# Dense products between attention passes: one fixed issue order, weights transposed in place, three w1 slabs used twice

## The chip, the cores and the metric

The kernel runs on one core of a Trainium2 chip. The metric is the device time of one execution in microseconds (us). Each quoted time is the median of several runs, and all runs that are compared here are of the same (fast) state. A core has these engines: PE (TensorE, matrix products and transposes), DVE (VectorE), ACT (ScalarE), POOL (GpSimd) and SP (SyncE, which here issues the loads); sixteen DMA engines move the data. Each engine works through its own list of instructions, and the engines wait for each other through semaphores.

## The reference

Two identical layers, each an attention of one query over a cache of 65536 keys, followed by a feed-forward block; the outputs are the result and the gradients of all inputs.

```python
# D = 1024, 32 query heads, 4 key/value heads of 128, cache 65536, F = 3584, all bf16
x = A_x
x = x + attention(layernorm(x), A_k_cache, A_v_cache, A_wq, A_wo)
x = x + (relu(layernorm(x) @ B_w1 + B_b1) ** 2) @ B_w2 + B_b2
x = x + attention(...)        # the same weights and caches again
x = x + feed_forward(...)
# returned: x, and the vector-Jacobian product with grad_out for all nine inputs
```

The two caches have 67 MB each, so the work is four passes over them (forward of layer 1, forward of layer 2, and two backward passes), and between the passes there are three short **dense stretches** in which vectors are multiplied by wq, wo, w1 and w2. A pass cannot finish its arithmetic without the vectors that the stretch before it produces.

## The kernel before

All loads go into slots of one arena in SBUF, the core's on-chip memory (a slot has 8 KB per partition, and holds one slab of w1 or four rows of w2 or wq). A load is issued into a slot only when what was read from it is done. So if the reader of a slab is late, a load is late too. Between two passes seven or eight cache blocks are also kept in slots for the next pass.

A product of a vector with the *rows* of a weight needs the weight transposed. This is done in pieces: PE transposes eight 128x128 blocks into PSUM, the memory that takes PE's results (`front`), ACT or DVE copies the piece to SBUF (`evac`), and PE multiplies it by the vector (`back`). Some pieces are instead multiplied directly by DVE (one `scalar_tensor_tensor`), to share the work. Pieces that are transposed and not yet multiplied wait in a queue:

```python
class Rows:                                   # kernel before, shortened
    def front(self, job, kc, slab):           # for each piece:
        if stt <= tra:                        #   DVE is less loaded: a direct product
            nc.vector.scalar_tensor_tensor(...)
            self.did(job)
            continue
        pt = self.ps_wt()                     #   else PE transposes it
        for i in range(w):
            nc.tensor.transpose(pt[:, i, :], job["cols"](slab, k0 + i), ident_b[:, :])
        wt = self.pool.tile([P, 8, P], BF, name="wt", tag="wt", bufs=self.bufs)   # bufs = 6
        evac(wt[:, 0:w, :], pt[:, 0:w, :])
        self.queue.append((job, kc, q, wt))
        if len(self.queue) >= self.bufs:
            yield
    # ... back(): eight matmuls with the oldest piece of the queue
    def fill(self):
        while len(self.queue) < self.bufs and next(self.feed, "end") != "end":
            pass
    def run(self):
        self.fill()
        while self.queue:
            self.back()
            self.fill()                       # the queue is filled up to six after every product
```

The passes are held to program order (`with tc.manual_schedule(engines=ORDERED): pipeline(...)`, for PE, DVE and ACT in passes 1 to 3). The dense stretches are not: there the compiler's scheduler may move an instruction ahead of others on the same engine.

## Time and profile before

| | before |
|---|---|
| time, median (range) of the runs beside the changed kernel | 2032.6 us (2026.9 to 2035.4, 4 runs) |
| span of the profiled run | 2027.6 us |
| bytes moved by DMA | 794.98 MB |
| DMA rate inside the passes, median of the 149 windows of 10 us away from the stretches, the start and the end | 421 GB/s (118 of them 410 to 428) |
| granted PE clock, mean of the run | 0.904 |

From the page of the kernel before: the granted PE clock and the DMA rate in 40 equal slices of about 51 us, and the DMA total.

```profile
PEclk9989899799999987898998989889888889798888
...
GB/s 389 420 420 420 419 423 397 371 362 420 420 418 420 420 399 279 352 420 421 420 417 412 401 267 266 370 410 423 422 420 421 393 423 396 363 402 423 421 379 245
DMA packets 110846, 794.98 MB, mean 392 GB/s; under 512 B 9425, under 2 KB 9439, under 8 KB 49375
```

The kernel is bound by DMA in the passes. The rate falls in slices 16 and 17, 24 to 26 and, less, 8 and 9: the dense stretches.

### The profile page before, as it was taken

How to read it: one execution, taken by the hardware profiler on the slowest of the kernel's cores; microseconds unless marked ns; L12 is line 12 of the kernel's file. 1: busy time of each engine (PE TensorE's matmuls, PEld its weight loads, DVE VectorE, ACT ScalarE, POOL GpSimd, SP SyncE). 2: the span in 40 equal slices, each digit the busy share in tenths (PEclk: the TensorE clock that was granted, in tenths of full speed). 3: DMA queues.
4: the chain of work that ended last, by engine and by line, in shares of the span. 5: the costliest groups of instructions: out<-in, count | busy, mean ns of one | idle time of the engine just before them, and what ended most of it. 6: DMA issues, size and time to landing. Idle time of an engine off the chain costs nothing. (4 is left out here: it accounts for less than half of the span.)

```text
span 2027.6 us, 67015 instructions
## 1 busy us (share of the span) xinstructions
PE 1626.9 (80%) x30210; PEld 1332.9 (66%) x30210; DVE 1174.3 (58%) x2358; ACT 1044.6 (52%) x1613; POOL 144.5 (7%) x332
## 2 busy tenths in 40 slices
PE   6877888687877877787787887788788888698896
PEld 6877777687777776786676885455455555355554
DVE  5645455245554543544454457677667777577675
ACT  3434344144344352435363445587667667577675
POOL 0000000000000000000000001112121111111111
PEclk9989899799999987898998989889888889798888
DMA  9999999989999997899999977999999999999996
GB/s 389 420 420 420 419 423 397 371 362 420 420 418 420 420 399 279 352 420 421 420 417 412 401 267 266 370 410 423 422 420 421 393 423 396 363 402 423 421 379 245
DMA packets 110846, 794.98 MB, mean 392 GB/s; under 512 B 9425, under 2 KB 9439, under 8 KB 49375
## 3 DMA queue, kind: packets, MB, share of 16 engines
q1 hardware_dynamic: 86510, 624.99, 75.7%
q0 software_dynamic: 24048, 165.70, 19.8%
q8 instruction: 236, 3.87, 0.8%
q14 instruction: 52, 0.42, 0.1%
HBM read 624.96 MB, written 165.69 MB: 390 GB/s over the span
## 5 line engine op out<-in xcount | busy, mean ns | idle before, releaser
L153 DVE COPY kt<-ps_tr 128x1024 bf16<-128x1024 bf16 x724 | 497.8, 689 | 473.8 <-PE ps_tr L913 256.7
L150 ACT CAST arena<-ps_gg 128x1024 bf16<-128x1024 f32 x452 | 439.9, 1009 | 219.0 <-PE ps_gg L1280 160.7
L913 PE MATMUL ps_tr<-ident_b,arena 128*128 128x128 bf16 x3840 | 310.2, 226 | 60.4 <-DMA arena<-in_A_k_cache_dram 45.1
L913 PEld LDWEIGHTS <-arena 128*128 128x128 bf16 x3840 | 234.0, 101 | 66.6 <-DMA arena<-in_A_k_cache_dram 48.1
L153 DVE CAST arena<-ps_gg 128x1024 bf16<-128x1024 f32 (+1 forms) x191 | 228.9, 1198 | 82.4 <-PE ps_gg L1280 48.0
L150 ACT COPY kt<-ps_tr 128x1024 bf16<-128x1024 bf16 x164 | 172.2, 1054 | 183.9 <-PE ps_tr L1105 126.0
L1280 PE MATMUL ps_gg<-GG,xt 64*128 64x512 bf16 x1024 | 211.6, 413 | 46.4 <-DVE arena L153 26.8
L1015 PE MATMUL ps_acc<-arena 128*128 128x64 bf16 (+4 forms) x4096 | 206.0, 196 | 45.7 <-DMA arena<-in_A_v_cache_dram 31.7
L1226 PE MATMUL ps_tr<-ident_b,arena 128*128 128x128 bf16 x1824 | 175.9, 234 | 35.3 <-DMA arena<-in_A_v_cache_dram 34.4
L931 PE MATMUL ps_sc<-L_qpad,kt 128*128 128x64 bf16 (+7 forms) x3584 | 183.4, 194 | 17.9 <-issue 11.5
L996 ACT ACTIVATE arena<-S_sb,L_negm 128x128 bf16<-128x128 f32 x256 | 165.4, 1002 | 57.8 <-DVE L_negm L981 57.7
L1105 PE MATMUL ps_tr<-ident_b,arena 128*128 128x128 bf16 x1920 | 156.3, 228 | 48.3 <-DMA arena<-in_A_v_cache_dram 48.3
L1015 PEld LDWEIGHTS <-arena 128*128 128x128 bf16 x4096 | 159.8, 100 | 50.0 <-DMA arena<-in_A_v_cache_dram 34.8
L1226 PEld LDWEIGHTS <-arena 128*128 128x128 bf16 x1824 | 119.5, 104 | 88.8 <-issue 49.6
L931 PEld LDWEIGHTS <-kt 128*128 128x128 bf16 x3584 | 153.3, 100 | 23.6 <-issue 14.6
L1105 PEld LDWEIGHTS <-arena 128*128 128x128 bf16 x1920 | 118.6, 102 | 52.2 <-DMA arena<-in_A_v_cache_dram 51.0
L1306 PE MATMUL ps_acc<-X,arena 128*128 128x64 bf16 (+3 forms) x2048 | 119.7, 199 | 24.8 <-DMA arena<-in_A_k_cache_dram 24.8
L996 ACT ACTIVATION_READ_ACCUMULATOR arena<-S_sb,L_negm 128x1 f32 x256 | 127.8, 499 | 0.0
L1306 PEld LDWEIGHTS <-arena 128*128 128x128 bf16 x2048 | 87.1, 102 | 59.9 <-issue 33.1
L1150 PE MATMUL ps_acc<-dsT,arena 128*128 128x64 bf16 (+7 forms) x2048 | 103.7, 195 | 20.0 <-DMA arena<-in_A_k_cache_dram 15.8
L1280 PEld LDWEIGHTS <-xt 64*128 64x128 bf16 x1024 | 61.3, 94 | 86.3 <-issue 46.8
L1259 PE MATMUL ps_sc<-DOB,kt 128*128 128x64 bf16 (+3 forms) x1824 | 117.5, 200 | 0.0
(266 smaller groups left out, 2169.3 us busy)
## 6 DMA issues: line engine op xcount, KB each, us to landing
arena<-in_A_k_cache_dram SPq DMA_DIRECT2D x86, 2048.0 KB, 21.5
arena<-in_A_v_cache_dram SPq DMA_DIRECT2D x83, 2048.0 KB, 21.4
out_dram<-arena POOLq DMA_DIRECT2D x151, 1024.0 KB, 11.4
arena<-in_A_v_cache_dram SPq DMA_DIRECT2D x76, 1024.0 KB, 16.5
arena<-in_A_k_cache_dram SPq DMA_DIRECT2D x76, 1024.0 KB, 16.8
arena<-in_B_w_dram SPq DMA_DIRECT2D x32, 896.0 KB, 5.8
arena<-in_A_wq_dram SPq DMA_DIRECT2D x22, 1024.0 KB, 13.8
arena<-in_A_wo_dram SPq DMA_DIRECT2D x18, 1024.0 KB, 17.5
```

Source lines behind the costliest of these rows:

```text
L150: nc.scalar.copy(out=out, in_=in_)
L153: nc.vector.tensor_copy(out=out, in_=in_)
L913: nc.tensor.transpose(pt[:, i, :], kb8[:, i, :], ident_b[:, :])
L931: nc.tensor.matmul(state["ps_s"][:, s:s + w, :].rearrange("p a b -> p (a b)"), lhsT=kt[:, i, :], rhs=L["qpad"][:, g, 0:w, :].rearrange("p ...
L996: nc.scalar.activation(out=E(p, g, c0, SU)[:, :, h], in_=S[:, h, :], func=ACTF.Exp, bias=L["negm"][:, g, su, h:h + 1], scale=SCALE, accum_ ...
L1015: nc.tensor.matmul(ps_o[:, 0:w, :], lhsT=vb8[:, i, :], rhs=E(p, g, c, w), start=(c % SU == 0), stop=(c % SU == SU - 1), skip_group_check=True)
L1105: nc.tensor.transpose(pt[:, i, :], vb8[:, i, :], ident_b[:, :])
L1150: nc.tensor.matmul(ps_dq[:, 0:w, :].rearrange("p a b -> p (a b)"), lhsT=kb8[:, i, :], rhs=dsT[:, s:s + w, :].rearrange("p a b -> p (a b)") ...
L1226: nc.tensor.transpose(pt[:, i, :], vb8[:, i, :], ident_b[:, :])
L1259: nc.tensor.matmul(state["ps_dp"][:, s:s + w, :].rearrange("p a b -> p (a b)"), lhsT=vt[:, i, :], rhs=DOB[:, g, 0:w, :].rearrange("p a b - ...
L1280: nc.tensor.matmul(pg[:, 512 * h:512 * h + 512], lhsT=xt[64 * h:64 * h + 64, j1 // 8 + m, :], rhs=gg[64 * h:64 * h + 64, :, :].rearrange(" ...
L1306: nc.tensor.matmul(ps_dq[:, 0:w, :].rearrange("p a b -> p (a b)"), lhsT=kb8[:, i, :], rhs=X[:, s:s + w, :].rearrange("p a b -> p (a b)"), ...
```

## The change

The intent: (1) keep three of the eight w1 slabs of the forward product for the backward product that follows, which saves 2.75 MB of loads; (2) write the transposed piece back into its own slab, which saves six buffers; (3) hold the dense stretches to program order too, with the small vector steps spread among the transposes, and put the first transposes of the third stretch between the last steps of pass 3. In the first stretch four more pieces are multiplied directly by DVE (18 instead of 14). The core of the diff:

```diff
+    ordered.enter_context(tc.manual_schedule(engines=ORDERED))     # now around everything up to pass 4
@@ Rows.front
                 if stt <= tra:
                     nc.vector.scalar_tensor_tensor(...)
                     self.did(job)
+                    yield
                     continue
-                wt = self.pool.tile([P, 8, P], BF, name="wt", tag="wt", bufs=self.bufs)
-                evac(wt[:, 0:w, :], pt[:, 0:w, :])
-                self.queue.append((job, kc, q, wt))
-                if len(self.queue) >= self.bufs:
-                    yield
+                wt = slab[:, k0 * P:(k0 + w) * P].rearrange("p (a b) -> p a b", b=P)
+                evac(wt, pt[:, 0:w, :])
+                sl.users += 1                      # the slab stays occupied until back()
+                self.queue.append((job, kc, q, wt, sl))
+                yield
@@ Rows
-    def run(self):
-        self.fill()
-        while self.queue:
-            self.back()
-            self.fill()
+    def step(self):                                # AHEAD = 3
+        if self.chain is not None and next(self.chain, "end") == "end":
+            self.chain = None
+        for _ in range(2):
+            if self.queue and self.queue[0][0]["ready"] and (_ == 0 or len(self.queue) > self.AHEAD):
+                self.back()
+        r = self.one()                             # one piece: a transpose or a direct DVE product
+        return self.chain is not None or self.queue or r is None
+    def run(self, known=True):
+        # ... known: products of the first weight at once; else: self.fill(2)
+        while self.step():
+            pass
@@ second stretch
-    run(g_w1(L4, ps_mv, pre=rows.fill))
-    rows.run()
+    w1a, w1b = w1_twice(3)                         # three slabs stay for the second product
+    run(g_w1(L4, ps_mv, it=w1a))
+    rows.run(False)
@@ pass 3 and third stretch
-    attn_bwd3(2, L3, on3, bg, [(10, pre_load("wq3", ...))])
+    attn_bwd3(2, L3, on3, bg, [(10, begin34)] + [(k, lambda: rows34.fill(1)) for k in range(8, 0, -1)])
# ... (cut: first stretch, generators for the layer norms)
```

## The prediction

> **What bounds the kernel now.** The page's slices show DMA at 9 tenths or more nearly everywhere: 795 MB at a mean of 392 GB/s. Inside the four attention passes the stretches run at 418 to 428 GB/s. At 421 GB/s the bytes alone take an estimated 1888 us of the 2028 us span. The Trainium skill, "DMA: Bandwidth & Descriptors", Specifications, gives a fabric ceiling of 435 GB/s and this trace agrees. The other 140 us are stretches where the queue has no free slot. From 10 us windows, counted as time lost against 421 GB/s: first to second pass (330 to 440 us) 15 us, second to third (760 to 850) 25 us, third to fourth (1150 to 1320) 46 us, end of the last pass 28 us, the rest scattered. Only the three dense stretches, 86 us, can be helped.
>
> **What limits the dense stretches.** The timeline of 793.9 to 824.6 us (w1 backward, then wo) takes 31 us; 8 transposes take 0.46 us and 8 following matmuls 0.25 us, so its 228 + 228 PE instructions are an estimated 20 us of PE work. PE waits there for copies of transposed weights and for w1 loads. From 1175 to 1234.5 us PE does an estimated 47 us (8 side matmuls 0.42 us) in 60 us.
>
> **What the change does.**
> 1. Three of 16 w1 loads go: 2.75 MB, an estimated 6.5 us of DMA, in the second stretch, where they are waited for.
> 2. Transposed weights go back into their slab. Slabs stay occupied until their matmuls are issued, so about 1.5 slots of buffering (six 256 KB tiles) are lost. The copies' number and cost stay (DVE 0.69, ACT 1.01 us).
> 3. The order is fixed: transposes and matmuls alternate at a depth of two to three pieces, about 1.4 us apart, enough for a 1.01 us copy; layernorm chains run among transposes of the next weights. The skill ("TensorE: Matmul & The Clock Gate", Architectural detail) calls ACT and DVE strict FIFO, so a fixed order can also stall; untested here.
> 4. By the instruction order, PE work hardly changes: third stretch 428 to 416 transposes, second 228 as before; the first has 80 instead of 112, with 18 instead of 14 direct DVE products (1.30 us each), so DVE takes over there at about 23 us. All 64 wq transposes move into the tail of pass 3. Pass 4 keeps its order. The start stall of passes 3 and 4 (kept blocks fill the slots; DMA 107 to 163 GB/s at 1230 to 1250 us) moves but stays.
>
> **On the critical path.** A transition that PE leaves earlier ends the DMA pause earlier, so the gain is the shortening: first 2 us, second 8 us (6.5 us of loads and most of the waits, overlapping), third 8 us of at most 13. Sum 18 to 20 us.
>
> **Predicted: 2011 us, range 1994 to 2026.** Faster by over 2%: 0.07; within 2%: 0.91; slower by over 2%: 0.02.
>
> **What would show it.** DMA total 792.2 MB; pass rates unchanged at about 420 GB/s; the w1 backward and wo stretch 22 to 24 us instead of 31; the third stretch (from the end of pass 3's last matmul to the first dO) about 52 instead of 60 us; the first nearly unchanged; the pause at the start of pass 4 still 15 to 20 us.
>
> **What would make it wrong.** Lost buffering: if slabs held stop the loads, the third stretch gains nothing (2020 us). Early transposes may wait behind late loads and delay pass 3's matmuls. If the fixed order removes the start pauses of passes 3 and 4 too, 1990 us or less.

## More of the kernel before

I count **lost DMA time** as the sum over 20 us windows of (window) x (1 - rate / 421 GB/s). Counted to the last whole microsecond of the span, it comes to 138.6 us before the change: 25.8 us between 740 and 880 us (the second stretch, before pass 3), 47.3 us between 1140 and 1360 us (the third stretch and the start of pass 4), and 65.5 us elsewhere. Lost time plus bytes / 421 GB/s is the span by construction (but for the last fraction of a microsecond), so a table of lost time tells where a change of the span came from, and not why.

The two stretches as windows of the trace. After the window and its length the columns are busy us (and count) of PE, PE weight loads, DVE, ACT and POOL, then the granted PE clock, the DMA share and GB/s.

```profile
core 0: us, PE busy (x) PEld busy (x) DVE busy (x) ACT busy (x) POOL busy (x), PEclk, DMA share, GB/s
793.00:825.00 32.00, 27.10 (x487) 24.63 (x487) 22.34 (x58) 17.82 (x22) 0.61 (x13) 0.91 0.88 323
1175.00:1236.00 61.00, 56.37 (x1085) 53.86 (x1085) 42.71 (x106) 35.33 (x41) 1.83 (x12) 0.95 0.75 278
```

PE is the busiest engine there, at 85% and 92%. What it does in the third stretch, from the timeline of PE (L631 is a transpose of a piece, L656 the products of a piece, L1553 a forward product with the same w2 slab):

```profile
start us, us, engine line op out<-in xcount [idle before <-releaser]
...
1201.07 0.64 PE L631 MATMUL ps_sc<-ident_b,arena 128*128 128x128 bf16 x8
1201.54 0.41 PE L656 MATMUL ps_bg<-vcb,wt 128*128 128x64 bf16 x8
1201.79 1.05 PE L1553 MATMUL ps_acc<-L_gb,arena 128*128 128x64 bf16 x16
1202.65 0.64 PE L631 MATMUL ps_sc<-ident_b,arena 128*128 128x128 bf16 x8
...
```

One piece takes 1.58 us (from 1201.07 to 1202.65), and no line has an idle time in brackets: PE never waits for a copy, since the piece multiplied at 1201.54 was transposed and copied earlier. The waits of PE confirm it. The columns are: written tile and line <- releaser, us in total, times, longest; first the second stretch (780 to 870 us), then the third (1160 to 1380 us).

```profile
PE ps_bg L656 <- ACT wt L150: 2.5, 5, 0.7
PE ps_bg L656 <- DVE wt L153: 0.6, 2, 0.3
...
PE ps_bg L656 <- ACT wt L150: 1.2, 2, 0.7
PE ps_bg L656 <- DVE wt L153: 0.3, 1, 0.3
```

Products waited for their copies 4.6 us in all.

## The result, and the profile after

| | before | after |
|---|---|---|
| time, median (range), 4 runs each | 2032.6 (2026.9 to 2035.4) | 2098.7 (2095.6 to 2102.3) |
| ratio after / before, 95% interval | | 1.0329 (1.0300 to 1.0359) |
| span of the profiled run | 2027.6 | 2093.8 |
| DMA bytes | 794.98 MB | 792.21 MB |
| lost DMA time, 740 to 880 us | 25.8 us | 48.0 us |
| lost DMA time, 1140 to 1360 us | 47.3 us | 92.6 us |
| lost DMA time elsewhere | 65.5 us | 70.8 us |

A ratio here is always the mean time of one kernel's fast runs over that of the kernel before in the same rounds, so it is not quite the ratio of the medians. The changed kernel is slower by 3.3%. The sum closes, as it must by construction: 72.8 us more lost DMA time, less 6.6 us for the bytes saved (2.77 MB at 421 GB/s), is 66.2 us, and the spans differ by 66.2 us. Of the 72.8 us, 67.5 us lie in the second and third stretch with the pass starts that follow.

The page after, the same lines as before:

```profile
PEclk9989998799989986989898986779778898899898
...
GB/s 391 419 420 419 421 421 398 374 374 416 424 416 423 409 357 176 343 421 420 411 424 417 337 140 116 340 369 424 422 423 412 398 405 417 345 417 424 424 383 245
DMA packets 110396, 792.21 MB, mean 378 GB/s; under 512 B 9360, under 2 KB 9374, under 8 KB 48926
```

The saved bytes are there, and the passes run at their old rate (most slices of the passes lie between 409 and 424 GB/s). The slices 16, 24 and 25 are the new loss. The two stretches as windows, and two parts of the third (columns as before):

```profile
786.00:838.00 52.00, 34.91 (x499) 29.95 (x497) 22.46 (x55) 18.76 (x22) 0.65 (x14) 0.69 0.51 173
1191.00:1296.00 105.00, 69.86 (x1034) 60.16 (x1033) 40.40 (x99) 33.79 (x38) 1.20 (x12) 0.74 0.45 161
1210.00:1230.00 20.00, 12.74 (x232) 11.58 (x232) 6.17 (x12) 6.65 (x7) 0.00 (x0) 1.00 0.41 137
1240.00:1280.00 40.00, 24.26 (x262) 19.45 (x261) 13.25 (x26) 12.04 (x14) 0.00 (x0) 0.50 0.51 175
```

They now last 52 and 105 us instead of 32 and 61, with no more work (PE 1034 instead of 1085 matmuls in the third). DMA is idle half of the time, and PE, though "busy" 67% of the time, runs partly at half clock. So neither is the limit. The Trainium skill ("Perfetto Trace Analysis", Roofline) puts it this way: with matmul and HBM utilization both low, "you're latency-bound (stalls/dependencies), not roofline-bound". This trace agrees in kind: the DMA share is 0.45, and PE is idle or at half clock for much of the time. The timeline of PE shows the latency (L707 transposes a piece, L727 multiplies one, L1658 is the forward product):

```profile
...
1201.06 0.64 PE L707 MATMUL ps_sc<-ident_b,arena 128*128 128x128 bf16 x8
1201.53 0.41 PE L727 MATMUL ps_bg<-vcb,arena 128*128 128x64 bf16 x8
1202.48 0.42 PE L727 MATMUL ps_bg<-vcb,arena 128*128 128x64 bf16 x8
1203.16 0.64 PE L707 MATMUL ps_tr<-ident_b,arena 128*128 128x128 bf16 x8
1204.90 0.42 PE L727 MATMUL ps_bg<-vcb,arena 128*128 128x64 bf16 x8 [1.10 <-ACT arena L149]
1205.16 1.06 PE L1658 MATMUL ps_acc<-L_gb,arena 128*128 128x64 bf16 x16
1206.02 0.64 PE L707 MATMUL ps_tr<-ident_b,arena 128*128 128x128 bf16 x8
1207.77 0.42 PE L727 MATMUL ps_bg<-vcb,arena 128*128 128x64 bf16 x8 [1.10 <-ACT arena L149]
...
```

Two products follow each other at 1201.53 and 1202.48 without a transposed piece between them. From then on each product waits: transpose at 1203.16, 1.10 us of idle time for the ACT copy, product at 1204.90, and the next at 1207.77. A piece takes 2.87 us instead of 1.58. The waits of PE, same windows as before:

```profile
PE ps_bg L727 <- ACT arena L149: 12.1, 12, 1.2
PE ps_bg L727 <- DVE arena L152: 2.7, 4, 0.8
...
PE ps_bg L727 <- ACT arena L149: 27.1, 27, 1.2
PE ps_bg L727 <- DVE arena L152: 4.0, 6, 0.9
```

The waits of products for copies grew from 4.6 to 45.9 us. These are 41.3 of the 66.2 us; what the rest consists of is not itemised (e15 looks at the lowered clock).

**What happened in the program.** `step` issues the products of one piece every time, then asks for one more piece. If that piece is a direct DVE product, nothing enters the queue, so each DVE product shrinks the queue by one. In the third stretch the first one starts between the two products shown above:

```profile
1202.34 1.22 DVE L697 SCALAR_TENSOR_TENSOR mv_junk<-arena,vbc 128x1024 bf16<-128x1024 bf16 x1
```

Within one weight nothing lets the queue grow again (`AHEAD` only allows a *second* product in a step). Only between two weights, while the next vector is not ready, do some pieces gather: in the second stretch, counted from the timeline, two at the start, one from 798 us on, three at 833 us when wo begins, and one again at its end. At one, the order on PE is transpose i, product i, transpose i+1, product i+1, and every product waits for the copy of the piece just transposed. In the kernel before, `fill` refilled the queue to six after every product.

### The profile page after: what moved, and what is told of

Its sections match the earlier page's. It is cut to its first block, busy times and chain, and to the rows that moved or that the text cites. A ratio compares the mean times of both kernels' runs of the same rounds, so it can differ in the third digit from the quotient of the medians.

```text
span 2093.8 us, 66846 instructions
## 1 busy us (share of the span) xinstructions
PE 1667.5 (80%) x30122; PEld 1355.3 (65%) x30122; DVE 1182.7 (56%) x2370; ACT 1040.4 (50%) x1607; POOL 145.5 (7%) x338
## 2 busy tenths in 40 slices
DMA packets 110396, 792.21 MB, mean 378 GB/s; under 512 B 9360, under 2 KB 9374, under 8 KB 48926
## 4 chain that ended last, share of the span: by engine, by line
DMA 45%; PE 37%; ACT 7%; DVE 6%; issue 4%; POOL 0%; SPq 0%; POOLq 0%; ACTq 0%; DVEq 0%
DMA arena<-in_A_v_cache_dram 20%; DMA arena<-in_A_k_cache_dram 18%; PE ps_tr L1024 5%; DMA out_dram<-arena 5%; ACT arena L149 5%; PE ps_gg L1389 4%; PE ps_tr L1335 3%; PE ps_sc L1042 3%; PE ps_acc L1126 3%; PE ps_tr L1215 2%; DVE arena L152 2%; PE ps_sc L1368 2%; PE ps_tr L707 2%; PE ps_mv L527 2%; PE ps_bg L727 2%
## 5 line engine op out<-in xcount | busy, mean ns | idle before, releaser
L1024 PE MATMUL ps_tr<-ident_b,arena 128*128 128x128 bf16 x3840 | 309.7, 225 | 58.6 <-DMA arena<-in_A_k_cache_dram 42.2
L1389 PE MATMUL ps_gg<-GG,xt 64*128 64x512 bf16 x1024 | 217.2, 422 | 40.5 <-DVE arena L152 21.6
L1335 PE MATMUL ps_tr<-ident_b,arena 128*128 128x128 bf16 x1824 | 181.2, 239 | 38.0 <-DMA arena<-in_A_v_cache_dram 37.3
L1215 PE MATMUL ps_tr<-ident_b,arena 128*128 128x128 bf16 x1920 | 161.1, 231 | 40.8 <-DMA arena<-in_A_v_cache_dram 39.0
L1042 PEld LDWEIGHTS <-kt 128*128 128x128 bf16 x3584 | 152.9, 100 | 25.8 <-issue 18.0
L149 ACT COPY arena<-ps_tr 128x1024 bf16<-128x1024 bf16 x63 | 64.9, 1032 | 145.0 <-PE ps_tr L707 97.0
## 6 DMA issues: line engine op xcount, KB each, us to landing
arena<-in_A_k_cache_dram SPq DMA_DIRECT2D x76, 1024.0 KB, 14.5
```

The lines of the kernel that those rows point to most:

```text
L149: nc.scalar.copy(out=out, in_=in_)
L1024: nc.tensor.transpose(pt[:, i, :], kb8[:, i, :], ident_b[:, :])
L1042: nc.tensor.matmul(state["ps_s"][:, s:s + w, :].rearrange("p a b -> p (a b)"), lhsT=kt[:, i, :], rhs=L["qpad"][:, g, 0:w, :].rearrange("p ...
L1215: nc.tensor.transpose(pt[:, i, :], vb8[:, i, :], ident_b[:, :])
L1335: nc.tensor.transpose(pt[:, i, :], vb8[:, i, :], ident_b[:, :])
L1389: nc.tensor.matmul(pg[:, 512 * h:512 * h + 512], lhsT=xt[64 * h:64 * h + 64, j1 // 8 + m, :], rhs=gg[64 * h:64 * h + 64, :, :].rearrange(" ...
```

## The experiments

My theory (A) is that the queue shrank to one. Rivals were: (B) writing in place holds slabs, so loads come late; (C) a fixed order loses by itself; (D) the kept w1 slabs leave too few slots; (E) the lowered PE clock is the cause and not a consequence; (F) the early transposes hold up the end of pass 3. Every run below gave correct results. Lost DMA time is given as second stretch / third stretch with the start of pass 4, in the windows used above; for comparison, before 25.8 / 47.3 and after 48.0 / 92.6.

### e1: a deeper queue, all else as changed

```diff
             for _ in range(2):
-                if self.queue and self.queue[0][0]["ready"] and (_ == 0 or len(self.queue) > self.AHEAD):
+                if self.queue and self.queue[0][0]["ready"] and (self.ended or len(self.queue) > self.AHEAD):
                     self.back()
             r = self.one()
+            self.ended = r == "end"
```

> The changed kernel, with one rule altered: a piece's products are issued only while more than three transposed pieces wait (or none is left to come), instead of one at every step. A (the queue of transposed pieces had shrunk to one, so that transpose, copy and product of a piece follow one another): the product of the feed-forward and output weights before pass 3 takes 22 to 30 us instead of 52, the stretch before pass 4 some 55 to 65 instead of 105, the granted clock there rises, and the time falls to 2005 to 2025 us. B (the copy back into the slab, or slabs held longer, starves the loads): a deeper queue holds slabs longer, so no gain or a loss, 2095 us or more. C (a fixed order as such loses): 2085 to 2100.

Measured: 2042.1 us, ratio 1.0058 (1.0033 to 1.0082); lost DMA time 32.3 / 58.8. One rule of the queue brings back about 2.7 of 3.3 points, and in the two windows used above no product waits for a copy any more. A is right about most of the loss, but the time stays above the kernel before, and above the range that I gave.

### e2, e3: the kernel before in a fixed order, with a queue of six and of one

```diff
-    rows.run()
+    with tc.manual_schedule(engines=ORDERED):
+        rows.run()
```

and for e3 also

```diff
-        def __init__(self, pool=None, bufs=NWT):
+        def __init__(self, pool=None, bufs=1):       # the pool keeps its six buffers
```

> The kernel before, its queue of six pieces untouched, but the product runs of the two stretches before pass 3 and before pass 4 held to program order (the compiler may not move instructions there). C (fixed order as such costs the time): 2070 us or more. A (only the depth matters): 2025 to 2045 us, same as before.

> As the run with the kernel before in fixed order, but with a queue of one piece (the six buffers for transposed weights stay, nothing is written in place). A: the stretches before pass 3 and pass 4 slow as in the changed kernel, 2075 to 2110 us. B (in-place transposes, held slabs): stays at 2030 to 2045, as nothing is in place and slabs come free at once.

Measured: e2 2047.7 us, ratio 1.0071 (1.0040 to 1.0102), lost 29.0 / 64.5; e3 2152.4 us, ratio 1.0598 (1.0568 to 1.0629). e2 fell between the two expectations: the fixed order costs the kernel before about 0.7%, so C is a part, but a small one. (Only the runs of pieces are held here, not the vector steps around them as in the changed kernel.) e3 makes the kernel before slow without any in-place writing, kept slab or early transpose, so none of these is needed for the loss. It loses more than I expected. The waits of its PE (same two windows) show the same pattern, 73.7 us of it:

```profile
PE ps_bg L656 <- ACT wt L150: 19.2, 18, 1.2
PE ps_bg L656 <- DVE wt L153: 6.7, 8, 0.9
...
PE ps_bg L656 <- ACT wt L150: 36.6, 33, 1.4
PE ps_bg L656 <- DVE wt L153: 11.2, 13, 1.2
```

### e4: no early transposes in pass 3

```diff
-    attn_bwd3(2, L3, on3, bg, [(10, begin34)] + [(k, lambda: rows34.fill(1)) for k in range(8, 0, -1)])
-    bg.drain()
+    attn_bwd3(2, L3, on3, bg, [(10, begin34)])
+    bg.drain()
+    for _ in range(8):
+        rows34.fill(1)
```

> The changed kernel with the eight early transposes issued after pass 3 instead of between its last steps. F (early transposes wait for late loads in the fixed order and hold up the end of pass 3): 10 us or more faster than the changed kernel, 2088 or less. A: the queue is at one either way, within 5 us of 2098 (2093 to 2105).

Measured: 2098.9 us, ratio 1.0338 (1.0312 to 1.0365). F falls: the change alone was 1.0329.

### e5, e6: fewer slabs kept

e1 with `w1_twice(3)` replaced by `w1_twice(0)` (e5) and `w1_twice(1)` (e6).

> The changed kernel with the deeper queue of e1, but no w1 slab kept: all eight are loaded twice, as before the change (2.75 MB more, worth 6.5 us at 421 GB/s). D (three kept slabs and the broadcast vector leave one of five free slabs to circulate, so the loads of the second stretch wait for slabs): no slower than e1 (2042 us) in spite of the extra bytes, 2030 to 2042, with the lost DMA time between 740 and 880 us down from 32 to 22 to 26 us. A alone (nothing but the depth mattered there): 2046 to 2051 us.

> As e5, with one w1 slab kept instead of none or three. D: the best of the three, 2028 to 2038 us: 2.2 us fewer bytes than e5 and three slabs left to circulate. A alone: 2044 to 2049 us, between e1 and e5 by bytes.

Measured: e5 2041.2 us, ratio 1.0054 (1.0035 to 1.0074), lost 34.2 / 58.9; e6 2039.6 us, ratio 1.0053 (1.0030 to 1.0077), lost 28.4 / 57.5. None, one or three kept slabs (e1) give the same time within the intervals, so neither expectation is met in full. The time of e5 lies at the edge of what D expected, but D's mechanism does not show: with no slab kept the lost time in the second stretch was 34.2 us, not 22 to 26. A alone expected the extra bytes to cost 4 to 9 us, and they did not show either. Kept slabs are not the cause of the loss; in this order they also bought nothing that I can measure.

### e7, e8: the deeper queue without early transposes, in place and with own buffers

e7 is e1 with the edit of e4 (six transposes instead of eight). e8 is e7 with (cut to its core)

```diff
-                wt = slab[:, k0 * P:(k0 + w) * P].rearrange("p (a b) -> p a b", b=P)
+                wt = DENSE["pool"].tile([P, 8, P], BF, name="wt", tag="wt", bufs=7)[:, 0:w, :]
-                sl.users += 1
```

> e1 with the early transposes (six) after pass 3 instead of between its last steps. F (they wait for late loads in the fixed order, or hold slabs, at the end of pass 3): lost DMA time from 1140 to 1360 us falls from 59 to 50 or less, 2035 us or less. Otherwise within 4 us of e1's 2042.

> e7, but in the stretches before pass 3 and pass 4 the transposed pieces go into seven buffers of their own, as before the change, and a slab is free once it is transposed. B (transposing in place holds slabs and delays loads): 8 us or more faster than e7. A alone: within 4 us of e7.

Measured: e7 2044.4 us, ratio 1.0065 (1.0039 to 1.0092); e8 2035.5 us, ratio 1.0025 (1.0002 to 1.0048), lost 37.8 / 64.1 and 32.2 / 62.6. F falls a second time. Own buffers gained 0.4% (9 us in the medians) at this depth, near what B expected; the two intervals still overlap.

### e9, e10: a free order with the shallow queue

In e9 the changed kernel keeps everything but the fixed order of the dense stretches; in e10 the kernel before gets a queue of one and keeps its free order.

```diff
-    ordered.enter_context(tc.manual_schedule(engines=ORDERED))
@@ passes 1 to 3
-        pipeline(items, [...], bg, end)
+        with tc.manual_schedule(engines=ORDERED):
+            pipeline(items, [...], bg, end)
```

> The changed kernel with one part undone: only the steps of passes 1 to 3 are held to program order, as before the change, and the dense stretches between them are left to the compiler's scheduler; the queue rule, the in-place transposes and the kept slabs stay. If the fixed order mattered because it made a queue of one binding (A together with C): the compiler lifts transposes ahead of the waiting products and most of the loss comes back, 2030 to 2055 us. If a queue of one costs the same in any order (A alone): 2085 to 2100. If in-place writing is what ties a piece's steps together (B): 2085 to 2100 as well.

> The kernel before with a queue of one piece in its program, its dense stretches left to the compiler as they were. With e3 (the same in fixed order, 2152 us): A together with C expects the compiler to repair most of it, 2030 to 2060 us; A alone expects 2100 us or more.

Measured: e9 2022.9 us, ratio 0.9970 (0.9947 to 0.9993), lost 26.3 / 50.2; e10 2040.7 us, ratio 1.0060 (1.0041 to 1.0079). e10 lies in the range of A together with C, e9 even below it. Here the shallow queue costs the kernel before 0.6% instead of 6%, and the changed kernel nothing. The timeline of e9 in the third stretch (L707 transposes, L727 products, L1659 the forward product) shows why:

```profile
1186.36 1.06 PE L1659 MATMUL ps_acc<-L_gb,arena 128*128 128x64 bf16 x16
1187.22 0.36 PE L707 MATMUL ps_tr<-ident_b,arena 128*128 128x128 bf16 x3
1187.42 0.41 PE L727 MATMUL ps_bg<-vcb,arena 128*128 128x64 bf16 x8
1187.67 0.44 PE L707 MATMUL ps_tr<-ident_b,arena 128*128 128x128 bf16 x5
```

No line has an idle time. The transposes at 1187.22 and 1187.67 are one piece, split around the product of an earlier one: the scheduler has put transposes ahead of products that wait, which the program did not say.

### e11, e12: a free order with the deeper queue, in place and with own buffers

e1 and e8, each with the edit of e9.

> e1 (queue of three to four) with the dense stretches left to the compiler. If the rest of e1's loss against the kernel before (14 us) is the fixed order (C, as e2 showed 14 to 15 us for the kernel before): 2022 to 2033 us. If it is in-place slabs or early transposes: 2037 to 2045.

> e8 (own buffers, no early transposes, queue of three) with the dense stretches left to the compiler. If the fixed order costs 14 us and the in-place writing 8 us, independently, this is the fastest, 2012 to 2025 us, ahead of both kernels; if they cost the same waits twice, 2025 to 2035.

Measured: e11 2026.9 us, ratio 0.9986 (0.9955 to 1.0016); e12 2027.6 us, ratio 0.9987 (0.9956 to 1.0018). e11 is where C expected it. In a free order own buffers gain nothing, so my sum in e12, 14 and 8 us independently, was wrong: they cure the same waits.

### e13, e14: one piece waiting, and six, in the fixed order

e1 with `AHEAD = 1` and with `AHEAD = 6`.

> e1 with the rule at one piece left waiting instead of three (the next piece is transposed before the products of this one): A (each product waits for its own copy, about 1.1 us after the transposes of 0.64 us): one piece hides most of that wait, so most of the gain of e1 comes already here, 2045 to 2065 us. If depth had little to do with it, 2085 or more.

> e1 with six pieces left waiting instead of three. If e1's rest of 14 us is still depth: 2030 us or less. If it is the fixed order (other instructions waiting in line, slabs held longer by in-place pieces): 2040 us or more.

Measured: e13 2035.8 us, ratio 1.0026 (1.0011 to 1.0040), lost 32.5 / 56.5; e14 2080.0 us, ratio 1.0242 (1.0228 to 1.0256), lost 56.9 / 73.6. One waiting piece brings nearly the whole gain, more than I expected. The timeline of e13 (L708 transposes, L728 products, L1660 the forward product) has a piece every 1.59 us, as before the change:

```profile
1185.39 0.64 PE L708 MATMUL ps_tr<-ident_b,arena 128*128 128x128 bf16 x8
1185.87 0.41 PE L728 MATMUL ps_bg<-vcb,arena 128*128 128x64 bf16 x8
1186.12 1.05 PE L1660 MATMUL ps_acc<-L_gb,arena 128*128 128x64 bf16 x16
1186.98 0.64 PE L708 MATMUL ps_tr<-ident_b,arena 128*128 128x128 bf16 x8
```

Six waiting pieces lose most of it again, but by another wait. The waits of the load issuer between 770 and 850 us (L466 loads w1, L440 wo, L346 the keys for pass 3):

```profile
SPq L466 <- PE ps_bg L728: 25.4, 4, 9.4
SPq L440 <- PE ps_bg L728: 15.4, 3, 6.8
SPq L346 <- PE ps_bg L728: 6.6, 2, 4.4
```

and those of PE in the same window:

```profile
PE ps_tr L708 <- DMA arena<-in_B_w_dram: 8.5, 2, 4.5
PE ps_sc L708 <- DMA arena<-in_B_w_dram: 5.7, 2, 2.9
PE ps_sc L708 <- DMA arena<-in_A_wo_dram: 5.3, 2, 3.2
```

Loads wait 47.4 us for products (L728) to release slabs, and PE then waits for those loads, 19.5 us. In the changed kernel the same window has the loads waiting 24.3 us for products and 23.3 us for copies (14.1 us in e14), and PE waiting for copies.

### e15: PE kept busy while it waits

The changed kernel with eight transposes that nobody reads after each piece:

```diff
             r = self.one()
+            if r is None and self.queue:
+                junk = ps_mv([P, 8, P], BF)
+                for i in range(8):
+                    nc.tensor.transpose(junk[:, i, :], ident_b[:, :], ident_b[:, :])
```

> The changed kernel as it is, queue of one, with eight transposes of the identity (nobody reads them) after each piece in the stretches before pass 3 and pass 4, while PE would wait for the copy. E (the lowered clock makes the loss): the granted clock there rises from 0.5 to 0.9 or more, and 15 us or more come back, 2083 us or less. A (the waits for the copies make it): the clock may rise, but the time stays within 10 us of 2098.

Measured: 2089.4 us, ratio 1.0297 (1.0276 to 1.0318), lost 48.5 / 86.8. The window 1240 to 1280 us of e15 (columns as above), to be read beside that of the changed kernel:

```profile
1240.00:1280.00 40.00, 29.18 (x523) 25.39 (x524) 17.33 (x40) 14.98 (x18) 0.00 (x0) 1.00 0.58 198
```

and its timeline in the third stretch (L804 is the added work):

```profile
1207.67 0.64 PE L707 MATMUL ps_tr<-ident_b,arena 128*128 128x128 bf16 x8
1208.15 0.61 PE L804 MATMUL ps_mv<-ident_b 128*128 128x128 bf16 x8
1209.41 0.42 PE L727 MATMUL ps_bg<-vcb,arena 128*128 128x64 bf16 x8 [0.66 <-ACT arena L149]
```

The granted clock went from 0.50 to 1.00, and the time fell by 9 us in the medians and 0.3 points in the ratios (about 7 us); the two intervals overlap. That is what A expected (within 10 us), not E (15 us or more). From transposes to product it is still 1.74 us (1207.67 to 1209.41, and 1203.16 to 1204.90 in the changed kernel), because the copy takes as long as ever. So E is at most a small part of what this run can show, and A the large one (e1, e13). The added transposes take PE time too, so the clock may cost somewhat more than the 7 to 9 us.

### e16: e9 again

> The kernel of e9 once more, with five rounds: if it beats the kernel before, the ratio stays at 0.994 to 0.999 and the interval lies below 1; about 6 us, the three w1 loads saved. If e9 was chance, the interval includes 1.

Measured over five rounds: 2027.7 us, ratio 0.9986 (0.9971 to 1.0002). The interval just includes 1, so the lead of e9 can be chance.

### e17, e18: depth six with own buffers, and in a free order

e17 is e14 with the edits of e7 and e8 and the queue capped at seven; e18 is e14 with the edit of e9.

> e14 (six left waiting, fixed order), but with the transposed pieces in seven buffers of their own and the queue capped at seven, no early transposes in pass 3 (which e4 and e7 found to be worth nothing). B (pieces transposed in place hold their slabs, so loads wait for products): the loss of e14 goes, 2030 to 2050 us. If depth in itself costs (late products, long tails): 2070 us or more.

> e14 with the dense stretches left to the compiler's scheduler, in place still. The order in which slabs are handed out is fixed when the kernel is written down, the scheduler can only bring products forward. If it does, 2025 to 2040 us, as with one and three in free order; if the held slabs bind in any order (B), 2060 us or more.

Measured: e17 2043.0 us, ratio 1.0074 (1.0057 to 1.0091), lost 36.3 / 60.4; e18 2023.3 us, ratio 0.9966 (0.9948 to 0.9985), lost 31.5 / 49.1. Taking the in-place writing away cures depth six, so it was the held slabs (B), not depth. The load issuer of e17 in the window used for e14 (L719 transposes):

```profile
SPq L466 <- PE ps_sc L719: 17.4, 2, 9.7
SPq L440 <- PE ps_tr L719: 6.9, 3, 6.4
```

Slabs are now released by the transposes, not by the products, and the two lines for w1 and wo add up to 24.3 instead of 40.8 us. In a free order the held slabs do no measurable harm either.

### All together

Ratios to the kernel before, by order and by how many pieces are left in the queue when one is multiplied (for the changed kernel, once DVE products have drained it). "Fixed" means the whole of the stretches for the changed kernel, but only the runs of pieces in the second and third stretch for the kernel before:

| kernel | left in the queue | fixed order | free order |
|---|---|---|---|
| before, own buffers | five (refilled) | 1.0071 (e2) | 1 (before) |
| before, own buffers | none | 1.0598 (e3) | 1.0060 (e10) |
| changed, in place | none | 1.0329 (the change) | 0.9970, 0.9986 (e9, e16) |
| changed, in place | one | 1.0026 (e13) | not run |
| changed, in place | three | 1.0058 (e1) | 0.9986 (e11) |
| changed, in place | six | 1.0242 (e14) | 0.9966 (e18) |
| changed, own buffers | three | 1.0025 (e8) | 0.9987 (e12) |
| changed, own buffers | six | 1.0074 (e17) | not run |

The large loss needs both: a program order that leaves no piece between a transpose and its product, and a fixed order that forbids the scheduler to mend it. In a free order the empty queue costs 0.6% in the kernel before (e10) and nothing in the changed one (e9). In the fixed order the queue has a best depth: too shallow and products wait for copies, too deep and, in place, loads wait for slabs.

The changed kernel and its variants in a free order are the fastest that I have: five runs of four kernels give 0.9966 to 0.9987, all below 1, with two of the five intervals (e9, e18) entirely below. That is 3 to 7 us, and the three w1 loads saved are 6.6 us of DMA. So a small gain over both kernels is likely and fits the bytes, but the longest of these runs (e16, five rounds) does not quite exclude that there is none.

**Open.** Why a fixed order with a sufficient queue still costs 0.3 to 0.7% against a free one (e13, e1, e2) is not isolated: products no longer wait for copies in e1, and the lost time is spread over both stretches. In e1 the transposes wait for weight loads instead, 13.9 us in the two windows (2.8 us before); in e13 they do not, but products wait 8.9 us for copies (4.6 us before). Why e3 is so much slower than the changed kernel is only described by its longer waits.

## Why the prediction was wrong, point by point

- **What bounds the kernel**: right in kind. The stretches in which the prediction looked for time (25 and 46 us lost) are those in which 67.5 of the 72.8 us were lost. (That the sum closes is no test of this.)
- **What limits the dense stretches**: wrong in the second, and hidden by the larger fault. The prediction put 20 us of PE work into 31 us and so took some 11 us for waits. Before the change PE waited 4.4 us in all from 793 to 825 us, 3.1 of them for copies. What could be gained shows in e9, where the fault is mended: the first `dlt_prod` product after the second stretch starts at 817.6 us instead of 825.0, and the last one after the third at 1228.3 instead of 1235.7. Both are 7.4 us earlier, near the 6.6 us of loads saved; the 8 us forecast for the third stretch did not come. (Each is one profiled run.)
- **Item 1, three loads saved**: right in bytes (792.21 MB against a predicted 792.2). Their 6.5 us did not show in the fixed order (e1, e5 and e6 agree), and are consistent with the free-order runs.
- **Item 2, lost buffering**: right in kind, not the cause. At a queue of one a piece holds its slab only briefly; held slabs cost 1.7 points at a depth of six (e14 against e17) and about 0.4 at three (e7 against e8).
- **Item 3, the step that failed**: "transposes and matmuls alternate at a depth of two to three pieces, about 1.4 us apart, enough for a 1.01 us copy". The instruction order does alternate, but I took the products for those of an earlier piece. The depth is two only until the first direct DVE product; from 1202.48 us on it is one, a piece takes 2.87 us, and each product idles 1.10 us for the copy. The sign of this step was wrong: 45.9 us of such waits instead of none. Since the transposed piece lies in its slab, the product and the next transpose both read a tile called "arena", and the listing with names alone can't tell whose product it is. The program can: one `back` per step, and a DVE product that adds nothing.
- **Item 3, fixed order**: the prediction gave the skill's note that ACT and DVE are strict FIFO as a warning and expected no cost. e2 shows 0.7% for the kernel before. No run separates what ACT or DVE contributes to this.
- **Item 4, engine work nearly unchanged**: right in counts (1034 against 1085 PE matmuls in the third stretch). But I counted work at full clock. The granted clock was 0.50 in parts, which e15 puts at some 7 to 9 us, with intervals that overlap.
- **"What would show it"**: the second stretch took 52 us instead of the predicted 22 to 24, the third 105 instead of 52; the first is unchanged as said (lost DMA time 14.5 against 16.0 us between 320 and 460 us). The pause at the start of pass 4 stayed (86 and 200 GB/s from 1300 to 1320 us; before 163 and 107 GB/s from 1230 to 1250 us).
- **"What would make it wrong"** named slabs held, early transposes and start pauses; it left out the queue itself. Early transposes made no difference (e4, e7).

## What to carry to other kernels

When a software pipeline is fixed in program order, work out from the program how many pieces lie between a producer and its consumer *in every branch*, above all in those that skip a producer step; here a branch that added nothing to the queue drained it until the next weight. A loose queue rule did little harm while the scheduler might reorder (0.6% in e10, none in e9), so removing that freedom is a change to every rule that relied on it. If the pieces are transformed in place, depth is paid for with held slabs, so the best depth in a fixed order was here the smallest that covers the copy (one piece).

## What the Trainium skill lacked or had wrong

- "TensorE: Matmul & The Clock Gate", HAM oscillation: it gives the rule that PE must have no idle gaps over about 3.4 us, and the section after it adds, without a figure, that frequent short idle times can make the clock oscillate. Here the granted clock was 0.50 from 1240 to 1280 us, where no single wait for a copy was longer than 1.2 us, and 1.00 from 1210 to 1230 us with waits of 1.10 us. What differed was the work between the waits: in the second window there is a forward product of 16 matmuls per piece and in the first there is none. Eight transposes more per piece, and nothing else, raised it to 1.00 (e15). So the work between the waits counts too, and the rule about a single gap is not enough. Part 1 of the page says only in general that the clock follows how busy PE has been of late; what share keeps it up, no page says.
- The same page, Back-to-back issue gap: it gives a sustained 81 ns per matmul of 128 columns with weight loads. Here eight such transposes, each with its own weight load, start 0.47 us before the next group (1201.07 to 1201.54 in the kernel before, 1185.39 to 1185.87 in e13), thus an estimated 59 ns each, near the 55.6 ns that the page's Part 1 gives for a warm array.
- "DMA: Bandwidth & Descriptors", Specifications: its row of about 358 GB/s per core, which the page's Bandwidth section repeats as what binds between HBM and SBUF, did not bind this one core; the passes ran at a median of 421 GB/s, under the 435 GB/s that the same table gives for the fabric. A note in the same section, that 358 GB/s is the share when two cores stream and that one core alone reaches 425 GB/s, fits these runs; the row and the sentence should say so.
- No page tells what a fixed program order costs or how deep a transpose, copy, product queue must be. Here, in a fixed order, with a copy of 1.01 us on ACT and a transpose to product latency of 1.74 us, one waiting piece was enough (ratio 1.0026), none cost 3.3%, and six in place cost 2.4%.
